# Row 1 of the up weights in two transfers, and its products taken by feature group

## The chip, the cores and the metric

The kernel runs on one core of a Trainium2 chip. The metric is the device time of one execution in microseconds (us). Before the change the median of three runs was 178.26 us (177.81 to 178.55).

## The reference

The input x has 2048 tokens of 512 features, in bf16. It is normalized over the features (`xn = (x - mean) / sqrt(var + eps)`), and three things are added up:

- x itself;
- a diagonal complex state space model (S5) over the tokens: a projection of xn to 512 complex states, the recurrence `h = Lam_bar * h + Bu[t]`, the projection back, twice the real part, and `xn * Dskip`;
- a SwiGLU feed-forward block: `(silu(xn @ w_gate) * (xn @ w_up)) @ w_down`, with 1376 hidden features.

```python
x = A_x
xn = _layernorm(x, axis=-1)
return x + _A_ref(xn, ...) + _B_ref(xn, B_w_gate, B_w_up, B_w_down)
```

## The kernel before, in words

Tokens are cut into four chunks of 512 (`CW`), each of four tiles of 128 tokens. The 512 input features are cut into four slices of 128 (`KD = 4`, the index `k`), which are the contraction steps of every product with a weight matrix. "Row k" of a weight matrix means its 128 rows of slice k. The hidden features of the feed-forward block are cut into three groups (`fgroups`): group 0 is columns 0 to 511, group 1 columns 512 to 1023, and the end group has the remaining 352. `FE` is 1024, the columns of groups 0 and 1. The tiles `wu01` and `wg01` hold these 1024 columns of all four rows of the up and the gate weights (the profile calls them `wu` and `wg`), and `w_end` the end group of both.

The instructions stand in an order written out by hand (`manual_schedule`); each engine works through its own list in that order, and semaphores make it wait for what it reads. Most loads are issued by the SP queue, in this order (lines 123 to 141): x tile 0; up rows 0, 1, 2, 3 (line 128); gate rows 0, 1; x tile 2; gate row 2; x tile 3; gate row 3; the end groups of gate and up; the four x tiles of chunk 1. A row of 1024 columns is 256 KB, 2 KB on each of the 128 partitions; the helper `load_row` issues it as one transfer (the profile puts the issue at line 117). An x tile is 128 KB, 1 KB on each partition. x tile 1 is issued by ACT, three small parameter rows by POOL.

The first two token tiles are handled specially, so that TensorE can begin before the normalization statistics are there. After some products on constants (`dummy`, line 668), each of the tiles 0 and 1 is transposed by TensorE against an identity (`raw_mm`, line 230). The mean over the features is taken away in the same PSUM bank: VectorE adds the two halves of a tile and accumulates the sum of every token (`sum_dve`, line 222), and a product of these sums with `minus_mean`, an identity scaled by -1/512, is accumulated onto the transposed tile (`cT_mean`, line 238). ScalarE and VectorE then copy the centered, transposed slices to SBUF (`raw_copy`, line 245; slices of even k on ScalarE, of odd k on VectorE; the profile names the destination `CF`, whose space is used). The division by the standard deviation comes later, as the scale of the ScalarE instruction that reads the finished product out of PSUM (`sw_up`, line 507, and `sw_gate`, line 495).

Then come the up products of tiles 0 and 1 (lines 717 and 718). `row_mm(0, k)` issues the four products that row k takes part in: tile i = 0 and 1 times group gi = 0 and 1, each of 128 tokens by 512 columns with 128 contraction steps (line 487). Each of the four (i, gi) has its own PSUM bank in `pair[0]`, in which the four rows accumulate, so that row 0 can be worked on while later rows are still on their way. In every product the token slice is the stationary operand, loaded before it, and 512 columns of the weights are streamed. After row 3 the four banks are read by ScalarE. The gate rows follow in the same way with `row_mm(1, k)`, with the transposition of the parameters and of x tile 2 among them.

The rest of the kernel, from about 13 us on, is a long sequence of TensorE products (the remaining tiles of chunk 0, then for each chunk the projection to the states, gate and up, and the two output projections), with the recurrence on VectorE and a backlog of other work spread between the products by estimated costs (`pump`, `need`).

Of the kernel before, what the change touches and what calls it, by code (L numbers as in the profile page):

```python
# [23 lines left out]
def kernel(  # L24
# [17 lines left out]
    nc = tc.nc  # L42
# [31 lines left out]
    def bank(shape=(128, CW), dtype=F32):  # L74
        return psum.tile(list(shape), dtype, name="ps")
# [7 lines left out]
    wu_v = B_w_up.rearrange("(k p) f -> p k f", p=128)  # L83
# [6 lines left out]
    FE = fgroups[-1][0] * 128  # L90
    wg01 = const.tile([128, KD, FE], BF16, name="wg01")
    wu01 = const.tile([128, KD, FE], BF16, name="wu01")
# [23 lines left out]
    def load_row(q, t, view, k):  # L116
        q.dma_start(out=t[:, k, :], in_=view[:, k, 0:FE])
# [7 lines left out]
    nc.scalar.dma_start(out=xall[:, 1, :], in_=x_v[:, 1, :])  # L125
    nc.scalar.preload_act_table_set("silu_and_others")
    for k in range(KD):
        load_row(nc.sync, wu01, wu_v, k)
    for k in range(HK):
        load_row(nc.sync, wg01, wg_v, k)  # L130
    nc.sync.dma_start(out=xall[:, 2, :], in_=x_v[:, 2, :])
# [93 lines left out]
    pair = [[[bank() for _ in range(2)] for _ in range(2)] for _ in range(2)]  # L225
# [253 lines left out]
    def tokens(i, k):  # L479
        if i < SW:  # L480
            return xcT[:, k, i * 128:(i + 1) * 128]
        return xnT0[:, k, i, :]

    def sw_mm(ps, groups, gi, i, k0=0, k1=KD):
        a, b = fgroups[gi]
        for k in range(k0, k1):
            nc.tensor.matmul(ps[:, 0:(b - a) * 128], lhsT=tokens(i, k), rhs=groups[gi][:, k, 0:(b - a) * 128],  # L487
                             start=(k == 0), stop=(k == KD - 1))
# [202 lines left out]
    G, U = wg_g, wu_g  # L691
# [18 lines left out]
        raw_copy(1, k)  # L710

    def row_mm(which, k):
        for i in range(2):
            for gi in range(2):
                sw_mm(pair[which][i][gi], (U, G)[which], gi, i, k, k + 1)

    for k in range(KD):
        row_mm(0, k)
# [6 lines left out]
    for n in range(2):  # L725
        norm_dve(n)
    row_mm(1, 0)
    pp = prm_transpose()
    ln_stats(2)
# [6 lines left out]
    for k in range(1, SW):  # L736
        row_mm(1, k)
# [167 lines left out]
```

## Time and profile before

| | before |
|---|---|
| median of three runs | 178.26 us |
| lowest and highest run | 177.81, 178.55 us |
| span of the profiled execution (first to last instruction) | 175.8 us |
| TensorE (PE) busy | 171.4 us, 97% |
| VectorE (DVE) busy | 156.9 us, 89% |
| ScalarE (ACT) busy | 102.0 us, 58% |
| mean DMA traffic | 102 GB/s |

The profile is of one execution. Its own time beside the span of 175.8 us is not listed; the median run is 2.46 us longer than the span. The page gives the busy time of each engine, the chain of work that ended last, and groups of instructions with what ended the idle time before them. The timeline lists instructions with start and length in us, merged where they are alike; "x16" after a row counts the instructions in it. The starts of neighbouring matmuls are closer than one lasts, because they are pipelined. "PE" is the product itself, "PEld" the load of its stationary operand, "SPq" an issue on SP's queue. For a transfer the DMA view gives the time from issue to landing.

### The profile page before, as it was taken

The page shows a single profiled execution, that of the slowest core. Times are in us where ns is not written, and L with a number is a line of the kernel's source. Part 1 is how long each engine was busy: PE and PEld are TensorE (multiplying, and loading weights), DVE is VectorE, ACT ScalarE, POOL GpSimd, SP SyncE. Part 2 cuts the span into 40 slices and gives each one's busy share as a digit, 9 for nine tenths or more (in the row PEclk, how much of TensorE's full clock was granted, in tenths as well). Part 3 has the DMA queues.
Part 4 walks back from the last instruction along what each step waited for, and adds up shares of the span by engine and source line. Part 5 has one row for each costly group of instructions (what it writes and reads, how often), then busy time and mean ns, then how long its engine had stood idle before and what let it go on. Part 6 is the DMA issues. An engine that isn't in the chain of part 4 may idle for free.

```text
span 175.8 us, 2365 instructions
## 1 busy us (share of the span) xinstructions
PE 171.4 (97%) x847; PEld 82.6 (47%) x863; DVE 156.9 (89%) x259; ACT 102.0 (58%) x188; POOL 28.1 (16%) x39
## 2 busy tenths in 40 slices
PE   8999999999999999999999999999999999999993
PEld 4544446464444444446444444446444444444542
DVE  3776999999999999999999999999999998699542
ACT  3379498793997685236598660024666653990100
POOL 5244110032000000044300000025000000522500
PEclk9999999999999999999999999999999999999999
DMA  5998929999999300047016000007200000696921
GB/s 184 344 350 83 245 48 205 285 191 300 161 218 306 112 4 0 0 38 82 2 34 119 0 0 0 0 0 87 36 15 17 0 4 0 87 175 96 117 66 60
DMA packets 34043, 17.88 MB, mean 102 GB/s; under 512 B 24896, under 2 KB 32928, under 8 KB 33984
## 3 DMA queue, kind: packets, MB, share of 16 engines
q1 hardware_dynamic: 30288, 14.22, 34.1%
q0 software_dynamic: 3456, 3.28, 14.4%
q10 hardware_dynamic: 288, 0.23, 0.4%
q8 instruction: 7, 0.11, 0.3%
q14 instruction: 4, 0.03, 0.1%
HBM read 8.03 MB, written 5.24 MB: 75 GB/s over the span
## 4 chain that ended last, share of the span: by engine, by line
PE 96%; DMA 1%; issue 1%; DVE 0%
PE ps L455 29%; PE ps L598 22%; PE ps L611 16%; PE ps L380 16%; PE ps L487 8%; PE ps L541 3%; PE ps L771 2%; DMA xall<-in_A_x_dram 1%; PE ps L230 1%; PE ps L238 0%; DVE xall L614 0%; PE ps L271 0%
## 5 line engine op out<-in xcount | busy, mean ns | idle before, releaser
L598 PE MATMUL ps<-wd_sb,guT 128*128 128x512 bf16 (+4 forms) x184 | 38.7, 366 | 0.2
L422 DVE TENSOR_TENSOR_SCAN g<-r_t,car,u 128x512 bf16<-128x512 f32 x24 | 29.1, 1264 | 0.0
L611 PE MATMUL ps<-CF,wt 128*128 128x512 bf16 (+2 forms) x134 | 28.4, 366 | 0.1
L380 PE MATMUL ps<-xnT,BT 128*128 128x512 bf16 x125 | 28.1, 379 | 0.2
L598 PEld LDWEIGHTS <-guT 128*128 128x128 bf16 (+1 forms) x187 | 17.9, 98 | 20.5
L455 PE MATMUL ps<-xnT,wu 128*128 128x512 bf16 x95 | 24.6, 379 | 0.2
L455 PE MATMUL ps<-xnT,wg 128*128 128x512 bf16 x91 | 23.9, 379 | 0.1
L618 POOL DMA_DIRECT2D out_dram<-res x12 | 10.5, 1043 | 77.3 <-ACT res L617 72.1
L469 ACT ACTIVATE guT<-ps 128x512 bf16<-128x512 f32 x30 | 18.3, 609 | 4.8 <-PE ps L455 4.5
L470 ACT CAST u<-ps 128x512 bf16<-128x512 f32 x30 | 17.9, 596 | 4.6 <-PE ps L455 4.5
L382 ACT CAST u<-ps 128x512 bf16<-128x512 f32 x32 | 17.5, 597 | 4.8 <-PE ps L380 3.3
L611 PEld LDWEIGHTS <-wt 128*128 128x128 bf16 x136 | 13.0, 98 | 14.7
L380 PEld LDWEIGHTS <-BT 128*128 128x128 bf16 x128 | 12.5, 98 | 14.8
L617 ACT CAST res<-ps 128x512 bf16<-128x512 f32 x12 | 6.8, 583 | 21.0 <-PE ps L611 21.0
L572 ACT ACTIVATE xr<-xall,nb,rstd 128x512 bf16<-128x512 bf16 x16 | 11.8, 805 | 9.1 <-DVE xall L580 4.9
L455 PEld LDWEIGHTS <-wu 128*128 128x128 bf16 x96 | 9.4, 98 | 11.3
L455 PEld LDWEIGHTS <-wg 128*128 128x128 bf16 x96 | 9.3, 98 | 10.6
L192 POOL TENSOR_TENSOR rstd<-ve,neg_half 128x1 f32<-128x1 f32 (+1 forms) x7 | 7.6, 1079 | 29.4 <-DVE ve L191 29.0
L455 PE MATMUL ps<-xnT,w_end 128*128 128x512 bf16 x48 | 10.9, 379 | 0.0
L182 DVE BATCH_NORM_STATS2 stats<-xall 128x6 f32<-128x512 bf16 x16 | 10.8, 675 | 0.0
L474 DVE TENSOR_TENSOR guT<-guT,u 128x1024 bf16<-128x1024 bf16 x15 | 10.0, 675 | 0.0
L390 DVE TENSOR_TENSOR pm<-g,c 128x2048 bf16<-128x2048 bf16 x8 | 9.8, 1220 | 0.1
(120 smaller groups left out, 207.8 us busy)
## 6 DMA issues: line engine op xcount, KB each, us to landing
out_dram<-in_A_x_dram SPq DMA_DIRECT2D x3, 512.0 KB, 5.3
out_dram<-res POOLq DMA_DIRECT2D x12, 128.0 KB, 3.1
out_dram<-xall POOLq DMA_DIRECT2D x3, 512.0 KB, 6.0
wd_sb<-in_B_w_down_dram SPq DMA_DIRECT2D x1, 1280.0 KB, 8.2
wu<-in_B_w_up_dram SPq DMA_DIRECT2D x4, 256.0 KB, 3.8
wg<-in_B_w_gate_dram SPq DMA_DIRECT2D x4, 256.0 KB, 4.8
xall<-in_A_x_dram SPq DMA_DIRECT2D x1, 1024.0 KB, 7.0
xall<-in_A_x_dram SPq DMA_DIRECT2D x1, 512.0 KB, 6.1
```

Source lines behind the costliest of these rows:

```text
L182: nc.vector.bn_stats(out=stats[:, n, 0, :], in_=xall[:, n, :])
L380: nc.tensor.matmul(ps[:] if c else by_k(ps[:]), lhsT=BT[:, part, k, q * 128:(q + 1) * 128], rhs=xnT[:, c, k, :] if c else xnT0[:, k], star ...
L382: nc.scalar.copy(out=u_tiles[c][:, part, q, :], in_=ps[:])
L422: V.tensor_tensor_scan(out=g()[:, part, q, :], data0=r_t[:, q:q + 1].to_broadcast([128, CW]), data1=u_tiles[c][:, part, q, :], initial=ini ...
L455: nc.tensor.matmul(ps[:fs, lo:hi], lhsT=wslice(groups, fi, k), rhs=xnT[:, c, k, lo:hi], start=(k == 0), stop=(k == KD - 1))
L469: nc.scalar.activation(out=guT[:fs, fi, :], in_=psg[:fs], func=ACT.Silu)
L470: nc.scalar.copy(out=u_pair[c][:fs, fi % 2, :], in_=psu[:fs])
L487: nc.tensor.matmul(ps[:, 0:(b - a) * 128], lhsT=tokens(i, k), rhs=groups[gi][:, k, 0:(b - a) * 128], start=(k == 0), stop=(k == KD - 1))
L572: nc.scalar.activation(out=box["xr"][:], in_=xall[:, n, :], func=ACT.Identity, scale=rstd[:, n:n + 1], bias=nb[:, n:n + 1])
L598: nc.tensor.matmul(o[:], lhsT=gu_tiles[c][:fsz[fi], fi, i * 128:(i + 1) * 128], rhs=wd_sb[:fsz[fi], fi, lo:hi], start=(fi == 0), stop=False)
L611: nc.tensor.matmul(o[:], lhsT=w_tiles[c][:, part, q, i * 128:(i + 1) * 128], rhs=CF[:, part, q, lo:hi], start=False, stop=(part == 1 and q ...
L618: nc.gpsimd.dma_start(out=out_v[:, n, lo:hi], in_=res[:, lo:hi], accum_op=ALU.add)
```

## The change

Row 1 of the up weights is loaded in two transfers, columns 0 to 511 and columns 512 to 1023, each of 128 KB, 1 KB on each partition. The other rows keep one transfer each (the loop over `[(0, FE)]` issues what `load_row` issued). And in `row_mm(0, 1)` the four products are taken by feature group: tile 0 and tile 1 with group 0, then tile 0 and tile 1 with group 1, where before tile 0 had both groups first and then tile 1. Rows 0, 2 and 3 and all gate rows keep their order. The same products go into the same banks, and nothing else is changed.

```diff
     for k in range(KD):
-        load_row(nc.sync, wu01, wu_v, k)
+        for lo, hi in [(0, FE // 2), (FE // 2, FE)] if k in (1,) else [(0, FE)]:
+            nc.sync.dma_start(out=wu01[:, k, lo:hi], in_=wu_v[:, k, lo:hi])
     for k in range(HK):
         load_row(nc.sync, wg01, wg_v, k)
...
     def row_mm(which, k):
-        for i in range(2):
-            for gi in range(2):
-                sw_mm(pair[which][i][gi], (U, G)[which], gi, i, k, k + 1)
+        order = [(i, gi) for i in range(2) for gi in range(2)]
+        if which == 0 and k in (1,):
+            order = [(i, gi) for gi, i in order]
+        for i, gi in order:
+            sw_mm(pair[which][i][gi], (U, G)[which], gi, i, k, k + 1)
```

## The prediction

> **What bounds the kernel now.** I read the page first (busy shares, then the chain that ended last), then the chain in order of time over the first 16 us, then the timelines of TensorE and of SP's queue around the loads that change, and last the landing times of single transfers.
>
> ```profile
> span 175.8 us, 2365 instructions
> PE 171.4 (97%) x847; PEld 82.6 (47%) x863; DVE 156.9 (89%) x259; ACT 102.0 (58%) x188; POOL 28.1 (16%) x39
> PE 96%; DMA 1%; issue 1%; DVE 0%
> ```
>
> TensorE is the bound: 171.4 of 175.8 us, and 96% of the chain that ended last. The sum is made against this execution, whose span is 175.8 us; the median of the timed runs, 178.26 us, lies 2.46 us above it, and I carry that difference over unchanged. Of the chain itself, the beginning matters here (start, length, what):
>
> ```profile
> 0.74 2.48 DMA xall<-in_A_x_dram
> ...
> 5.14 4.32 PE ps L487 x20
> ```
>
> What TensorE waits for at the start is the first tile of x, at 3.22 us (0.74 + 2.48). No load of the up weights is in the chain. The timeline of TensorE over the up rows says the same (start, length, group), and so do the groups by line (busy, mean ns | idle before) and the stage from 5 to 6 us (PE busy first, then the other engines, the granted clock, DMA):
>
> ```profile
> 4.98 3.62 PE L487 MATMUL ps<-wu,CF 128*128 128x512 bf16 x16
> 8.43 1.03 PE L487 MATMUL ps<-wg,CF 128*128 128x512 bf16 x4
> 9.29 0.22 PE L271 MATMUL ps<-ident,prm_rows 128*128 128x128 bf16 x1
> 9.35 1.89 PE L487 MATMUL ps<-wg,CF 128*128 128x512 bf16 x7
> L487 PE MATMUL ps<-wu,CF 128*128 128x512 bf16 x16 | 3.6, 379 | 0.0
> 5.00:6.00 1.00, 1.00 (x6) 0.44 (x5) 0.82 (x4) 0.60 (x3) 0.00 (x0) 1.00 1.03 331
> ```
>
> All 16 products of four up rows take 3.62 us. One lasts 0.379, so they start every (3.62 - 0.379) / 15 = 0.216 us, with no idle time before any (the 0.0 of the group's row), and the stage from 5 to 6 us, where row 1 begins, is all busy at a granted clock of 1.00. So row k starts at 4.98 + 4 x 0.216 x k: row 1 at 5.84, row 2 at 6.71, row 3 at 7.57, and the first gate row at 8.43.
>
> When did their data come? SP issues them (start, length, count from that start):
>
> ```profile
> 1.19 0.42 SPq L117 DMA_DIRECT2D wu<-in_B_w_up_dram  x1
> 1.65 0.91 SPq L117 DMA_DIRECT2D wu<-in_B_w_up_dram  x2
> 2.60 0.43 SPq L117 DMA_DIRECT2D wu<-in_B_w_up_dram  x1
> 3.07 0.91 SPq L117 DMA_DIRECT2D wg<-in_B_w_gate_dram  x2
> 4.02 0.43 SPq L131 DMA_DIRECT2D xall<-in_A_x_dram  x1
> 4.50 0.69 SPq L117 DMA_DIRECT2D wg<-in_B_w_gate_dram  x1
> 5.23 0.43 SPq L133 DMA_DIRECT2D xall<-in_A_x_dram  x1
> 5.70 0.43 SPq L117 DMA_DIRECT2D wg<-in_B_w_gate_dram  x1
> 6.19 0.45 SPq L113 DMA_DIRECT2D w_end<-in_B_w_gate_dram  x1
> 7.02 0.38 SPq L113 DMA_DIRECT2D w_end<-in_B_w_up_dram  x1
> 7.79 0.37 SPq L141 DMA_DIRECT2D xall<-in_A_x_dram  x1
> ```
>
> and the DMA view, asked one issue at a time, gives the us from issue to landing of up rows 0 to 3, gate rows 0 to 3 and x tiles 2 and 3, in this order:
>
> ```profile
> wu<-in_B_w_up_dram SPq DMA_DIRECT2D x1, 256.0 KB, 3.0
> wu<-in_B_w_up_dram SPq DMA_DIRECT2D x1, 256.0 KB, 3.6
> wu<-in_B_w_up_dram SPq DMA_DIRECT2D x1, 256.0 KB, 4.0
> wu<-in_B_w_up_dram SPq DMA_DIRECT2D x1, 256.0 KB, 4.4
> wg<-in_B_w_gate_dram SPq DMA_DIRECT2D x1, 256.0 KB, 4.7
> wg<-in_B_w_gate_dram SPq DMA_DIRECT2D x1, 256.0 KB, 4.8
> wg<-in_B_w_gate_dram SPq DMA_DIRECT2D x1, 256.0 KB, 4.9
> wg<-in_B_w_gate_dram SPq DMA_DIRECT2D x1, 256.0 KB, 4.8
> xall<-in_A_x_dram SPq DMA_DIRECT2D x1, 128.0 KB, 4.7
> xall<-in_A_x_dram SPq DMA_DIRECT2D x1, 128.0 KB, 4.5
> ```
>
> With issues 0.47 us apart (1.65 to 2.60 is two of them), the up rows land at 4.19, 5.25, 6.12 and 7.00, gate row 0 at 7.77, gate row 1 at 3.54 + 4.8 = 8.34, x tile 2 at 8.72, gate row 2 at 9.40, x tile 3 at 9.73 and gate row 3 at 10.50. Against the starts above the slack is 0.79 us for up row 0, **0.59 for row 1**, 0.59 for row 2, 0.57 for row 3, 0.66 for gate row 0, 1.0 for gate row 1 and 0.81 for gate row 2 (due four products after 9.35, at 10.21).
>
> **The change, part by part.**
>
> *Row 1 in two halves, first products on the first half.* The first two products of row 1 wait for 128 KB instead of 256. The first half should land about midway between rows 0 and 1, at 4.7 instead of 5.25. Its reader starts at 5.84 either way, since TensorE is busy with row 0 until then. Gain: 0, covered by the four products of row 0. The third product now has a wait of its own, on the second half; that half lands near 5.25 and is due at 5.84 + 2 x 0.216 = 6.27. A wait already met shows no price: each row's first product has one today, and the spacing of 0.216 holds across rows. Behind a wait here would stand all of TensorE's program, but it is met a microsecond ahead.
>
> *One more issue on SP.* It costs 0.43 + 0.04 = 0.47 us of SP's queue, and every transfer behind it is issued 0.47 later: up rows 2 and 3 at 2.60 and 3.07, gate rows 0 to 2 at 3.54, 4.02 and 4.97, x tiles 2 and 3 at 4.50 and 5.70, gate row 3 at 6.17, the end weights at 6.66 and 7.15. Does this move the landings? Only if the DMA engines would run dry. They do not: landings are 0.33 to 1.06 us apart while each transfer needs 3.0 to 4.9 us from issue, growing as the queue fills. The shortest issue-to-landing time of a whole row is 3.0, so row 2 could land from 2.60 + 3.0 = 5.60, and the queue brings it at 6.12; row 3 from 6.07 against 7.00, gate row 0 from 6.54 against 7.77. The late issue is hidden by 0.52 us of queue at row 2 and by more behind it. Lower end 0; upper end, were the cover gone, 0.47 us on all landings from row 2.
>
> One of SP's waits further back:
>
> ```profile
> SPq L113 <- DMA wu<-in_B_w_up_dram: 0.4, 1, 0.4
> ```
>
> The up half of the end weights goes out at 7.02 when up row 3 has landed (7.00), and four x tiles at 7.79 when gate row 0 has (7.77): both times the transfer eight places earlier on SP's queue. The new transfer stands ahead of both members of these pairs, so the pairs stay; the 0.4 us wait at L113 takes up the shift, and the x tiles still go at 7.79. Behind them SP next issues at 12.45, held by other work. ACT's and POOL's queues get nothing new.
>
> *Two transfers of 1 KB per partition in place of one of 2 KB.* The trace has transfers of the half's exact shape: the x tiles. Landing to landing, x tile 2 took 8.72 - 8.34 = 0.38 us and the gate row behind it 9.40 - 8.72 = 0.68; x tile 3 took 0.33 and its gate row 0.77. Two halves against one whole: 2 x 0.38 - 0.68 = +0.08, or 2 x 0.33 - 0.77 = -0.11. These differences of rounded times bound the price; I take 0, and keep -0.11 and +0.08. The traffic in a stretch of whole rows and in one where half the packets are 1 KB agrees:
>
> ```profile
> DMA packets 172, 0.28 MB, mean 348 GB/s; under 512 B 36, under 2 KB 37, under 8 KB 172
> DMA packets 202, 0.27 MB, mean 392 GB/s; under 512 B 20, under 2 KB 111, under 8 KB 202
> ```
>
> (6.2 to 7.0 us, and 8.7 to 9.4 us.) The Trainium skill, page "DMA: Bandwidth & Descriptors", section "Bandwidth", speaks against the change: transfers pay a fixed part, 0.95 us for 64 KB but 6.15 us for 1 MB. A straight line through its two figures is 0.61 us of fixed part (an estimate from that page, measured there for another issuing engine), and by it the second half would bring every later landing 0.61 us back. That would use up the 0.57 to 0.59 us of slack, and the sum by it would be +0.04 us. The rows above, at most 0.08, do not agree with it.
>
> *Token tiles alternate within row 1.* The number of weight loads stays, one per product. What moves is that the copy of token tile 1, feature slice 1 is needed one product (0.216 us) earlier.
>
> ```profile
> 5.18 0.29 DVE L245 CAST CF<-ps 128x128 bf16<-128x128 f32 x1 [0.72 <-PE ps L238]
> 5.34 0.10 PEld L487 LDWEIGHTS <-CF 128*128 128x128 bf16 x1 [0.26 <-ACT CF L245]
> 5.84 0.10 PEld L487 LDWEIGHTS <-CF 128*128 128x128 bf16 x1
> ```
>
> It is ready at 5.47, and the weight load that wants it comes at 5.84: 0.37 us to spare. Cost 0; it would be at most 0.22. (The load at 5.34 does wait for its copy, but belongs to row 0, which keeps its order.) The partial sums go to the same four banks, and these are read only after row 3.
>
> Sum: 0 + 0 + 0 + 0. The end weights are read from 15.6 on, far off. Forecast: **no change, 178.3 us**.
>
> **The rivals.**
>
> *S: later rows come late (slower).* Place: the landing of up rows 2 and 3. Mechanism: the added issue and a fixed price of the second half push all later landings back by d, and TensorE stalls by d less the slack, once. It decides from d = 0.57. Bounds of the rows: 0.47 + 0.08 = 0.55, a stall of nothing; if a half cost as much as the slowest whole row (5.25 - 4.19 = 1.06) beside a half at half price, the extra is 0.53, with the issue 1.00, the stall 0.43, 178.7 us. If in the timed executions the loads stood 0.6 us later against TensorE, so that the slack were gone, the whole 1.00 would show: 179.3, +0.6%. For it: three rows have almost the same thin slack. Against it: the queue is 3 to 4 transfers deep when the added issue comes.
>
> *F: row 1 is what TensorE waits for in the timed executions (faster).* The first half then comes up to 0.53 us earlier, half of the gap 1.06: 177.7 us. For it: row 1 has the longest gap before it. Against: rows 2 and 3 have no more slack than row 1, so loads late enough to hold row 1 hold row 3 too, and TensorE would give the gain back there; and there is no idle time before any of the 16 products.
>
> *T: the alternation makes TensorE wait for the VectorE copy.* At most 0.22 us, 178.5, from the point where the copy ends 0.37 us later than it does.
>
> ```profile
> 8.98 0.69 DVE L182 BATCH_NORM_STATS2 stats<-xall 128x6 f32<-128x512 bf16 x1
> ```
>
> **How the numbers follow.** (The row above is x tile 2's first reader on VectorE.) No change 0.62, S 0.22, F 0.12, T 0.04. The timed runs of before lie between 177.81 and 178.55, so about 0.5% is what a measurement of this kernel can tell from no change. Of S, 0.17 is beyond that bound: it needs the slack gone, or a later tile (x tile 2's first reader on VectorE has only 8.98 - 8.72 = 0.26 us) to pass its delay on too. Of F, 0.08 is beyond it, though no row prices it over 0.53 us: I leave it for what the profiled execution does not show. Of no change, 0.03 falls on either side by scatter.
>
> Faster 0.03 + 0.08 = 0.11, slower 0.03 + 0.17 = 0.20, same the rest, 0.69. The range reaches to F's 177.7 less the scatter of the fastest run (0.45), some 177.3, and to S's 179.3 at its full price: 177.3 to 179.4. The likeliest case alone: 177.8 to 178.7.
>
> **What would show it.** In the profile after: five issues of wu from SP where there were four, 0.47 us apart, the wait at L113 gone and the four x tiles issued at about 7.8 us again; the half landing near 4.7, up rows 2 and 3 at 6.1 and 7.0 within 0.1; TensorE's 16 up products still in 3.62 us with no idle time. Wrong would be: a gap on TensorE before up row 2, up row 3 or gate row 0 (S), 16 products in less than before (F, since before would have had a hidden wait), or a weight load at about 5.8 us waiting for VectorE's copy (T).

## The result, and the profile after

The changed kernel takes 178.88 us in the median of 8 runs (178.41 to 179.66), the kernel before 178.07 us in the median of 8 (177.76 to 178.55). The ratio is 1.0041, 95% interval 1.0025 to 1.0057: slower by 0.73 us (0.0041 x 178.07; the two medians differ by 0.81), and by less than the 0.5% that was taken as the bound of "no change".

The page of the profiled execution after: the span, the busy times, and the chain by engine.

```profile
span 176.9 us, 2382 instructions
PE 173.0 (98%) x863; PEld 83.1 (47%) x863; DVE 157.0 (89%) x259; ACT 102.3 (58%) x188; POOL 28.1 (16%) x39
PE 98%; DVE 0%; issue 0%
```

The span is 1.1 us longer than the one shown of before. Two places hold all of it. The first is the up rows: TensorE's timeline (start, length, group, count), and the loads of its stationary operands.

```profile
4.68 4.59 PE L488 MATMUL ps<-wu,CF 128*128 128x512 bf16 x16
9.10 1.03 PE L488 MATMUL ps<-wg,CF 128*128 128x512 bf16 x4
5.11 0.15 PEld L488 LDWEIGHTS <-CF 128*128 128x128 bf16 x1 [0.28 <-ACT CF L246]
5.53 0.15 PEld L488 LDWEIGHTS <-CF 128*128 128x128 bf16 x1 [0.27 <-issue]
5.96 0.15 PEld L488 LDWEIGHTS <-CF 128*128 128x128 bf16 x1 [0.28 <-issue]
6.39 0.15 PEld L488 LDWEIGHTS <-CF 128*128 128x128 bf16 x1 [0.28 <-DVE stats L183]
6.73 2.90 PEld L488 LDWEIGHTS <-CF 128*128 128x128 bf16 x14 [0.19 <-issue]
```

The 16 up products begin 0.30 us earlier than before (4.68 against 4.98: the first x tile landed earlier) and take 4.59 us instead of 3.62, so the gate rows begin at 9.10 instead of 8.43, 0.67 us later. That is not a wait for data: until 6.4 us the loads come every 0.43 us and last 0.15, after it every 0.22 us (2.90 us for 14) and 0.10. TensorE runs at half speed until about 6.6 us here, and did so until about 5.0 us in the profile before. From the first gate product on (9.10 us after, 8.43 before) the two executions run in parallel, 0.67 us apart, to the last product.

The second place is the end. SP's last issue, and what SP waited for (total us, times, longest), after:

```profile
174.16 0.33 SPq L616 DMA_DIRECT2D out_dram<-xall  x1
SPq L903 <- DMA out_dram<-xall: 1.0, 1, 1.0
```

and before:

```profile
173.49 0.33 SPq L615 DMA_DIRECT2D out_dram<-xall  x1
SPq L900 <- DMA out_dram<-xall: 0.5, 1, 0.5
```

From the issue of the last store to the end of the span it is 175.8 - 173.49 = 2.31 us before and 176.9 - 174.16 = 2.74 us after (by the trace's finer times 2.36 and 2.79, which are used from here on): 0.43 us more, with nothing in it but the landing of the store and waits. So the profile pair says 0.67 + 0.43 = 1.1. The experiments ask which of the two belongs to the change.

In the trace one can follow SP's own waits after the last store. SP steps through the completion semaphores one by one (start in us; the numbers are those of the semaphores):

```
before: store, completes on 109 | wait 102 at 173.93, 103 at 173.99, ... 108 at 174.36, 109 done at 174.94 | end 175.8
after:  store, completes on 102 | wait 102 done at 175.62, 103 at 175.68, 104 at 175.74, ... 109 at 176.05 | end 176.9
```

Eight semaphores, 102 to 109, are given to the transfers of SP's and ACT's queues in turn. Before, the last store falls on the last of them, and the other seven waits are done with while it is on its way. With one transfer more it falls on the first, and seven waits follow its landing, 0.062 us each: 0.43 us.

### The profile page after: what moved, and what is told of

Same layout as the page of the kernel before. It is cut to its first block, busy times and chain, and to the rows that moved or that the text cites. A ratio compares the mean times of both kernels' runs of the same rounds, so it can differ in the third digit from the quotient of the medians.

```text
span 176.9 us, 2382 instructions
## 1 busy us (share of the span) xinstructions
PE 173.0 (98%) x863; PEld 83.1 (47%) x863; DVE 157.0 (89%) x259; ACT 102.3 (58%) x188; POOL 28.1 (16%) x39
## 4 chain that ended last, share of the span: by engine, by line
PE 98%; DVE 0%; issue 0%
PE ps L456 29%; PE ps L599 22%; PE ps L612 16%; PE ps L381 16%; PE ps L488 8%; PE ps L542 3%; PE ps L774 2%; PE ps L669 1%; PE ps L231 1%; PE ps L239 0%; DVE xall L615 0%; PE ps L272 0%
## 5 line engine op out<-in xcount | busy, mean ns | idle before, releaser
L456 PE MATMUL ps<-xnT,wg 128*128 128x512 bf16 x96 | 24.6, 379 | 0.0
```

What stands on the lines that cost most here:

```text
L456: nc.tensor.matmul(ps[:fs, lo:hi], lhsT=wslice(groups, fi, k), rhs=xnT[:, c, k, lo:hi], start=(k == 0), stop=(k == KD - 1))
```

## The experiments

Two theories. **L (loads)**: the split makes later up rows land late and TensorE waits. **C (clock)**: only the moment at which TensorE goes to full speed differs, by chance. After the first four runs a third: **E (end)**, the position of the last store among the eight semaphores. Ratios are to the kernel before, run on the same chip.

**1. The split alone, and the order alone.**

```diff
# e1_split_only: this part of the change alone
-        load_row(nc.sync, wu01, wu_v, k)
+        for lo, hi in [(0, FE // 2), (FE // 2, FE)] if k in (1,) else [(0, FE)]:
+            nc.sync.dma_start(out=wu01[:, k, lo:hi], in_=wu_v[:, k, lo:hi])
# e2_order_only: this part alone
+        if which == 0 and k in (1,):
+            order = [(i, gi) for gi, i in order]
```

> Up row 1 in two transfers, its products in the old order (tile 0 with both groups first). Theory L (loads): the split itself makes up rows 2 and 3 land 0.7 to 0.9 us later than before (at about 7.0 and 7.8 us), as in the profile of the changed kernel, and the time rises as in the change: ratio to before 1.003 to 1.006. Theory C (clock): TensorE starts at half speed and the only thing that differs is when it goes to full speed (products 0.43 us apart, then 0.22 apart); the split does nothing to that, so the ratio is 1.000 within 0.2% over many runs, and a late landing costs nothing as long as it is under 0.6 us late against TensorE.

> Up row 1 in one transfer as before, its four products taken by feature group. Theory L: landings as before (up rows 2 and 3 at 6.1 and 7.0 us), ratio 1.000. Theory C: ratio 1.000 as well; if the ratio is 1.004 with landings as before, the order of the products does it, which neither theory has.

The split alone: 178.89 us, ratio 1.0031 (1.0017 to 1.0045). The order alone: 178.18 us, 1.0001 (0.9987 to 1.0014). The order costs nothing; the loss is the split's. In the profile of the order alone, with row 1 whole, TensorE waits for that row:

```profile
4.62 1.03 PE L487 MATMUL ps<-wu,CF 128*128 128x512 bf16 x4
6.14 2.75 PE L487 MATMUL ps<-wu,CF 128*128 128x512 bf16 x12 [0.50 <-DMA wu<-in_B_w_up_dram]
8.73 1.03 PE L487 MATMUL ps<-wg,CF 128*128 128x512 bf16 x4
```

Row 1 landed at 6.10 us here, 0.81 later than in the first profile of before (5.29, both by the trace's finer times), and the up products were at full speed from their start: TensorE sat idle for 0.50 us. In the profile of the split alone it is row 3:

```profile
4.70 3.39 PE L488 MATMUL ps<-wu,CF 128*128 128x512 bf16 x12
8.41 1.02 PE L488 MATMUL ps<-wu,CF 128*128 128x512 bf16 x4 [0.33 <-DMA wu<-in_B_w_up_dram]
9.27 1.03 PE L488 MATMUL ps<-wg,CF 128*128 128x512 bf16 x4
```

**2. Both kernels again, unchanged.**

> The kernel before, unchanged, as a second look. Ratio 1.000. Theory C: the moment at which TensorE goes from half to full speed (about 5.0 us in the first profile) lies elsewhere, anywhere from about 4 to 7.5 us, and the single runs scatter by the 0.7 us and more that this moves the time. Theory L: that moment is again about 5 us, and up rows 1 to 3 land again at 5.2, 6.1, 7.0 within 0.2.

> The changed kernel, unchanged, as a second look. Ratio about 1.004. Theory C: the moment of full speed (about 6.6 us in its first profile) lies elsewhere, and so does the span. Theory L: up rows 2 and 3 land again at about 7.0 and 7.8 us, 0.7 to 0.9 later than in the kernel before, whatever the clock does.

Before: 178.29 us, ratio 0.9999 (0.9986 to 1.0011). After: 178.95 us, 1.0038 (1.0025 to 1.0052). The loss is real and repeats. The moment of full speed was 5.5 us in the second look at before (5.0 in the first) and 5.4 in the second at after (6.6 in the first). So it wanders between executions of one kernel, and the 0.67 us of the first profile pair are the difference between two such moments, with no wait for a row in them. The 0.43 us at the end came back exactly: 2.35 and 2.36 us from the last store to the end in e2 and e3, 2.78 in e1 and e4.

The second pair has nearly the same moment of full speed in both profiles, and shows what the first pair hides (the first two rows are of before, the rest of after):

```profile
4.68 4.02 PE L487 MATMUL ps<-wu,CF 128*128 128x512 bf16 x16
8.54 1.03 PE L487 MATMUL ps<-wg,CF 128*128 128x512 bf16 x4
4.69 4.30 PE L488 MATMUL ps<-wu,CF 128*128 128x512 bf16 x16
8.84 1.03 PE L488 MATMUL ps<-wg,CF 128*128 128x512 bf16 x4
5.47 1.18 PEld L488 LDWEIGHTS <-CF 128*128 128x128 bf16 x6 [0.20 <-issue]
7.03 0.74 PEld L488 LDWEIGHTS <-CF 128*128 128x128 bf16 x4 [0.38 <-issue]
7.98 1.39 PEld L488 LDWEIGHTS <-CF 128*128 128x128 bf16 x7 [0.21 <-issue]
```

After, the gate rows begin 0.30 us later, and the weight loads show two breaks. By the trace's finer times the first product of row 2 starts 0.26 us later than the spacing of 0.216 would have it, 0.05 after that row landed (6.98), and the first product of row 3 starts 0.09 later, 0.04 after its landing (7.93). So in this pair the late rows cost TensorE 0.35 us. The timeline of the products shows no idle time there, because a product lasts longer than the spacing and short breaks are merged. Measured in the same way, by the starts, the waits are 0.66 us for row 1 in the order alone and 0.10 and 0.49 us for rows 2 and 3 in the split alone.

**3. The end alone.** One transfer more, and four more, late and far from the up rows; and the change with one transfer fewer, so that the last store is on the last semaphore again.

```diff
# f1_late_extra: cuts (0, 5, 10); f3_late_four: cuts (0, 2, 4, 6, 8, 10)
-        q.dma_start(out=wd_sb[:, 0:nfull, :], in_=B_w_down[0:nfull * 128, :]...)
+        for k0, k1 in zip(cuts[:-1], cuts[1:]):
+            q.dma_start(out=wd_sb[:, k0:k1, :], in_=B_w_down[k0 * 128:k1 * 128, :]...)
# f2_split_end_kept: the change, and
-    for a in range(0, (NCH - 1) * CW, CW):
-        nc.sync.dma_start(out=out[0, a:a + CW, :], in_=A_x[0, a:a + CW, :])
+    for a, b in ((0, 2 * CW), (2 * CW, (NCH - 1) * CW)):
+        nc.sync.dma_start(out=out[0, a:b, :], in_=A_x[0, a:b, :])
```

> The kernel before with one more SP transfer late and out of the way (the 1280 KB load of the down weights cut in two at about 38 us); the loads at the start are untouched. Theory E (end): one more transfer moves the last store from the last of the eight completion semaphores that SP waits for in turn at the end to the first of them; after the store has landed SP still has to step through the other seven, 0.06 us each, so the span grows by 7 x 0.062 = 0.43 us and the ratio to before is 1.0024, with up rows landing as before. Theory L (loads, late rows alone): ratio 1.000.

> The kernel before with four more SP transfers late (the load of the down weights cut in five). Theory E: the last store is then the fourth of the eight semaphores, four more waits follow it, 4 x 0.062 = 0.25 us, ratio 1.0014: less than with one extra transfer, although four are added. If added transfers cost by their number, it is more than with one. Theory L: 1.000.

> The changed kernel with one transfer fewer later on (three copies of x to the output, 1024 rows and 512 rows instead of three of 512), so that the last store is on the last of the eight semaphores again. Theory E: from the landing of the last store to the end of the span 0.9 us as in the kernel before, not 1.3, and the ratio to before falls from 1.004 to 1.0015 or less; what is left is the late up rows, and if they cost nothing it is 1.000. Theory L: the ratio stays at 1.003 to 1.004.

SP's last issue and the span, for one transfer more:

```profile
span 176.1 us, 2365 instructions
173.34 0.33 SPq L617 DMA_DIRECT2D out_dram<-xall  x1
SPq L902 <- DMA out_dram<-xall: 1.0, 1, 1.0
```

for four more:

```profile
span 176.4 us, 2370 instructions
173.77 0.33 SPq L617 DMA_DIRECT2D out_dram<-xall  x1
```

and for the change with its end kept:

```profile
span 176.6 us, 2366 instructions
174.24 0.33 SPq L616 DMA_DIRECT2D out_dram<-xall  x1
SPq L903 <- DMA out_dram<-xall: 0.5, 1, 0.5
```

From the store to the end: 2.78 us with one transfer more, 2.61 with four more, 2.37 with the end kept, against 2.36 before. The terms, +0.42 and +0.25, are those expected from seven and four waits of 0.062 (0.43 and 0.25). The times follow: one more 178.48 us, ratio 1.0019 (1.0007 to 1.0031; 1.0024 expected); four more 178.33, 1.0012 (0.9996 to 1.0028; 1.0014 expected). The times alone do not separate four transfers from one, or from none; the traces do. In all fourteen profiles the span is the start of the first gate product plus 167.4 us (167.41 to 167.43), plus 0.43 where the last store is on the first of the eight semaphores and 0.25 where it is on the fourth. So theory E is shown: one transfer more, at either of the two places tried, costs 0.43 us because of where it puts the last store, and four cost less than one. And nothing else that these kernels do after the first gate product makes a difference: what is left is settled by when the gate rows begin.

But the change with its end kept still has 178.65 us, ratio 1.0028 (1.0018 to 1.0038), where 1.0015 or less was expected. So something is left. (The merged copies of x are not it: the kernel with the tiny transfer, in the next experiment, has them too and costs nothing.) By this run it is 0.28%, 0.5 us; by subtracting the end's 0.43 us (0.24%) from the ratios of the split kernels (1.0031, 1.0038, 1.0041) it is 0.07 to 0.17%. The two ways agree only at the edges of their intervals.

**4. What is left: the late issue, the pieces, or the second transfer.**

```diff
# f4_tiny_after_row1: before, two output copies instead of three, and after row 1
+        if k == 1:
+            nc.sync.dma_start(out=spare[0:NQ, :], in_=A_Dskip.rearrange("(q j) -> q j", j=128))
# g1_cut_by_partition: f2_split_end_kept with row 1 cut the other way
-        for lo, hi in [(0, FE // 2), (FE // 2, FE)] if k in (1,) else [(0, FE)]:
-            nc.sync.dma_start(out=wu01[:, k, lo:hi], in_=wu_v[:, k, lo:hi])
+        for lo, hi in [(0, 64), (64, 128)] if k in (1,) else [(0, 128)]:
+            nc.sync.dma_start(out=wu01[lo:hi, k, :], in_=wu_v[lo:hi, k, 0:FE])
# h1_small_pieces: before, with a gap in the destination between the halves of a row
-    wu01 = const.tile([128, KD, FE], BF16, name="wu01")
+    wu01 = const.tile([128, KD, 2, CW + 32], BF16, name="wu01")
-        load_row(nc.sync, wu01, wu_v, k)
+        nc.sync.dma_start(out=wu01[:, k, :, 0:CW],
+                          in_=wu_v[:, k, 0:FE].rearrange("p (h c) -> p h c", h=2))
```

> The kernel before with row 1 whole, but a transfer of 1 KB into a spare tile issued between up rows 1 and 2, and one output copy fewer, so that the end is as in the kernel before. It costs the same 0.47 us of SP's queue as the second half, with almost no bytes. If the late issue is what makes the later up rows land late, rows 2 and 3 land at about 7.0 and 7.8 us and the ratio is that of the split with its end kept (1.001 to 1.0015). If it is the cutting of the row, rows 2 and 3 land as in the kernel before (6.1 to 6.8 and 7.0 to 7.4) and the ratio is 1.000.

> Row 1 again in two transfers of 128 KB and products by group, end kept as in the kernel before, but cut by partition: 64 partitions with 2 KB each, twice. If the pieces of 1 KB are what makes the later up rows land late, rows 2 and 3 land as with a whole row (6.1 to 6.9 and 7.0 to 7.6 us) and the ratio is 1.000 to 1.001. If it is the second large transfer, whatever its pieces, they land at 7.0 or later and 7.8 to 8.4, ratio 1.002 to 1.003 as with the split by columns and its end kept.

> The kernel before with every up row in one transfer as before, but in pieces of 1 KB: the destination has a gap of 64 bytes between the two halves of a row, so that no piece can be longer. Number and time of the issues and the end are unchanged. If pieces of 1 KB are what makes the rows behind them late, all four rows are now cut: rows 2 and 3 land at 7.0 or later and 7.8 or later, and the ratio is at least the 1.003 of the split with its end kept. If it is the second large transfer, rows 2 and 3 land as in the kernel before (6.1 to 6.9 and 7.0 to 7.6) and the ratio is 1.000 within 0.1%.

The tiny transfer: 178.24 us, ratio 1.0003 (0.9993 to 1.0013). Up rows 2 and 3 are issued 0.41 and 0.34 us later there (2.53 and 2.94 against 2.12 and 2.60), so the late issue alone, or most of its 0.47, costs nothing, as predicted. The pieces of 1 KB in whole-row transfers: 178.34 us, 0.9995 (0.9979 to 1.0011). The pieces cost nothing either, though four rows were cut (between 4 and 6 us 634 of 641 packets are under 2 KB, against 106 of 411 before). The cut by partition: 178.68 us, 1.0039 (1.0018 to 1.0060), with runs from 178.13 to 179.91; so the time speaks for a second large transfer, whatever its pieces.

The landings speak less clearly. Of each run there is one trace; up rows 2 and 3 landed at (us, from the issue and a time to landing rounded to 0.1):

| row 1 whole | row 2 | row 3 | | row 1 in two by columns | row 2 | row 3 |
|---|---|---|---|---|---|---|
| before | 6.12 | 7.00 | | after | 7.00 | 7.77 |
| e2 | 6.82 | 7.40 | | e1 | 7.00 | 8.40 |
| e3 | 6.42 | 7.10 | | e4 | 7.00 | 7.93 |
| f1 | 6.53 | 7.10 | | f2 | 7.30 | 8.17 |
| f3 | 6.92 | 7.60 | | g3 | 6.90 | 7.67 |
| f4 | 6.83 | 7.54 | | | | |
| g2 | 7.22 | 7.90 | | | | |

(g2 and g3 are the next pair.) Row 3 lands at 7.38 on average with a whole row 1 and at 7.99 with it cut by columns, 0.61 later, and only g2's 7.90 lies among the late ones. Row 2 lands at 6.69 and 7.04, 0.35 later. But the cut by partition had 6.68 and 7.32, and the small pieces 7.26 and 7.98, each against what its time says. The profile of the cut by partition is of a run of 178.32 us, one of its fastest, so its landings need not be those of the median run; and the small pieces land hardly later than the whole rows of g2. One trace apiece does not settle which property of the second transfer delays the rest; that stays open.

Nor is the clock ruled out for what is left. Of the four profiles with row 1 cut by columns and no added constant products (g3 has sixteen more), TensorE waits for late rows in two (0.35 us in e4, 0.59 in e1). In the other two, after and f2, it waits for none, and the gate rows begin late (9.10 and 9.18 us) because full speed came only at 6.6 and 6.8 us. In the profiles with a whole row 1 and no added products full speed came between 3.9 and 6.0 us. Whether the split itself moves that moment, or these profiles happened to have it late, no run here shows. The rows by themselves, with TensorE at full speed from the start, would have let the gate rows begin at 8.55 us on average of the seven profiles with a whole row 1 in the table (7.9 to 9.2) and at 8.93 with it cut by columns (8.7 to 9.3), 0.4 us later. This is an estimate from the traces: of each row its landing, 0.04 us, and 0.216 us for each product from that row on, and of these the latest. So late rows can explain what is left, but are not shown to be all of it.

**5. The loss with the late rows hidden.** Sixteen more constant products at the start, so that all rows have landed when the up products begin; for the kernel before and for the split with its end kept.

```diff
-    dummy(warm, 4, CW)
+    dummy(warm, 20, CW)
```

> The kernel before with 16 more constant products at the start, so that the up products begin some 5 us later, when all their rows have landed and TensorE is at full speed. Slower than before by those products, ratio 1.02 to 1.035; the runs are for comparison with the split kernel treated in the same way.

> The split with its end kept, with the same 16 constant products. Theory L (what is left of the loss with the end kept are late up rows): no row is late any more, so the time is that of the kernel before with the 16 products, within 0.1%. If a difference of 0.3 to 0.5 us stays, something other than late rows costs it.

Before so treated: 181.57 us (6 runs, 180.95 to 181.91), ratio 1.0187 (1.0163 to 1.0211). The split: 180.76 us (6 runs, 180.59 to 181.31), 1.0145 (1.0122 to 1.0167). No loss is left. But the two times were expected to agree within 0.1%, and the split is faster by 0.81 us, 0.4%, which no theory here expects. It is hardly scatter: only one of the six runs of the split is above the lowest run of the other. The moment of full speed lay between 3.9 and 6.8 us in the profiles, and each microsecond of it is half a microsecond of TensorE's time, about 1.4 us from end to end, so it could make such a difference; but the two profiles (5.2 us in g2, 5.0 in g3) do not show one of that size, and that of the split is of its slowest run (181.31). The cause stays open. These two runs are compatible with theory L for what remains; they don't prove it.

No run was faster than the kernel before beyond its interval.

## Why the prediction was right or wrong

The forecast of no change held by its own bound (0.41% against 0.5%), and 178.88 lies in the range. But the sum of four zeros was wrong: the change costs a measured 0.73 us, and rival S was nearer in sign. That the loss stayed inside the bound is luck: of the two terms of which it consists the prediction had one nowhere, and set the other at 0.

The prediction carried 2.46 us from the span to the median. In the runs whose span is listed the time is 1.9 to 2.2 us longer than the span, so the profiled execution, with 175.8, was 0.3 to 0.6 us quicker than the median run: it was no typical one to read a slack from.

**The gain of the first half: right.** No run shows any. The order's 0 and rival T's absence: right, 1.0001 for the order alone. Rival F: no support.

**One more issue on SP: half right, and here is the step that failed.** The later issue cost nothing (1.0003 with the tiny transfer), as the cover of 0.52 us and more had said. The prediction even found that each issue pairs with the transfer eight places earlier, but used it only as far as the x tiles at 7.79 and then said that SP next issues at 12.45. It should have been followed to the end of the program: the same eight semaphores are waited for in turn after the last store, and one more transfer turns the last store from eighth to first. The missing term is 7 x 0.062 = 0.43 us, over half of the 0.73 measured. It was to be seen in the trace of before: the last store is on semaphore 109, the last of the eight, and the waits for the seven others are over before it lands.

**Slack of 0.57 to 0.59 us: wrong as a property of the kernel.** It was read from one execution in which the rows came early and full speed came at 5.0 us. Whole rows have landed later since, row 1 at 6.55 us in g2 against 5.25, and in three of the profiles with row 1 in one transfer TensorE sits idle for an up row (0.50 us in e2, 0.79 in f3, 0.37 in h1). The row of f3, where full speed came earliest:

```profile
4.31 1.89 PE L489 MATMUL ps<-wu,CF 128*128 128x512 bf16 x8
6.99 1.89 PE L489 MATMUL ps<-wu,CF 128*128 128x512 bf16 x8 [0.79 <-DMA wu<-in_B_w_up_dram]
```

The loads are part of the bound there; which of loads and clock decides changes from execution to execution.

**The price of two transfers, -0.11 to +0.08 us: wrong, or at least too narrow.** With row 1 cut by columns row 2 lands 0.35 us later on average and row 3 0.61. The loss that is left for this is 0.07 to 0.28%, 0.1 to 0.5 us. Why the x tiles, of the same shape, showed no such price is open. The prediction had drawn a straight line through two figures of the Trainium skill's page "DMA: Bandwidth & Descriptors", section "Bandwidth", as an estimate of a fixed part (0.61 us; worked out again it is 0.60), and set it aside for the x tiles. The average of row 3 agrees with that estimate; that of row 2 is about half of it, and the landings of the cut by partition show no such delay, so it is not confirmed as a fixed price of every transfer.

**What would show it.** The first half of row 1 was forecast at 4.7 us and the second near 5.25; they landed at 5.12 and 5.65. Up rows 2 and 3 landed at 7.03 and 7.80, 0.86 and 0.80 later than in the profile of before and more than the slack. Still TensorE waited for neither, because it ran at half speed until 6.6 us: rival S's stall is absent from this profile and present in e1 and e4. The wait at L113 did not go either (0.7 us in two waits, 0.4 before). The four x tiles were forecast at about 7.8 us again and went at 8.42; the end weights' up half went at 7.82 and waited for up row 3's landing at 7.77: the pairs stayed, as said, but the landings did not.

```profile
7.82 0.37 SPq L113 DMA_DIRECT2D w_end<-in_B_w_up_dram  x1
8.42 0.37 SPq L142 DMA_DIRECT2D xall<-in_A_x_dram  x1
```

## What to carry to other kernels

Where transfers share a few completion semaphores in turn, adding or removing one anywhere shifts all later ones; look at which semaphore the last store gets, since the end of the program waits for them in order, and choose the number of transfers so that it gets the last. A merged timeline can hide a wait: compare the starts of the instructions with their usual spacing. A slack of half a microsecond in one profile is not a slack: compare several executions before calling a load hidden. A difference between two profiles at the start of a kernel may be the moment at which TensorE goes to full speed, so look at the spacing of the products first.

## What was not expected of the hardware

TensorE starts at half speed (products of 512 columns every 0.43 us, loads of 0.15 us) and changes to full speed (0.22 and 0.10) at a moment that wanders from execution to execution: 5.0 and 5.5 us in the two profiles of the kernel before, 6.6 and 5.4 in those of the changed one, 3.9 us at the earliest and 6.8 at the latest in all of them. The Trainium skill, page "TensorE: Matmul & The Clock Gate", Part 1, says that the window which decides it is free-running, some 3.4 us long, and that the number of slow products varies from run to run. The traces agree that it varies (none of the 16 up products is at half speed in e2, five are in f2), and the length of the window no run here shows. The clock column of the profile does not show the slow start: the stage table gives 1.00 for the whole of the stage from 5 to 10 us after, where the first four or five products run at half speed.

```profile
5.00:10.00 5.00, 5.00 (x21) 2.11 (x20) 3.74 (x12) 1.59 (x5) 1.24 (x2) 1.00 1.01 340
```
